# Memory read-out of an attention kernel: from one 128-row matmul per step to one 64-row matmul per head

## The chip, the cores and the metric

The kernel runs on one core of a Trainium2 chip. The metric is the device time of one execution in microseconds (us), lower is better. The profile comes from one profiled execution; the times of unprofiled executions are given beside it. The engines are named as in the profile: PE is TensorE (matmul and transpose), PEld its weight load, DVE is VectorE, ACT is ScalarE, POOL is GpSimd, SP is SyncE, which only issues DMA here.

## The reference, cut to what matters

Attention with a compressive memory, then two MLP layers on its output. B = 4, H = 8, S = 576, D = 64; 2304 tokens of width 512; the hidden width is 2048.

```python
scores = scale * q @ k.transpose(0, 1, 3, 2)            # causal mask, softmax -> a
local = a @ v
q_p = phi(q)                                            # elu(q) + 1
mem_ret  = einsum('bhsd,bhde->bhse', q_p, M_prev)       # the memory read-out:
mem_norm = einsum('bhsd,bhd->bhs', q_p, z_prev) + 1e-6  # 64 columns and one more
mem_out = mem_ret / mem_norm
attn = g * mem_out + (1 - g) * local                    # g = sigmoid(beta) per head
x = attn.transpose(0, 2, 1, 3).reshape(2304, 512)
x = silu(x @ moe_w_in) @ moe_w_out                      # layer 0
y = mish(x @ moe2_w_in) @ moe2_w_out                    # layer 1
```

## The kernel before

**Attention.** The 32 heads are taken as 16 pairs; the two heads of a pair (e = 0, 1) share the 128 partitions, 64 each, as q and k lie transposed. Queries come in tiles `qt` of 128 (the last, qt = 4, has 64). A visit is a pair with the tiles 0 and 1, or with 2, 3 and 4; the 32 visits make 80 steps (pair, qt), 64 with 128 queries and 16 with 64. A step has three parts. `stage_a` writes the scores to two PSUM banks (fp32 matmuls on 64 rows, one for each head), takes the softmax's exponent and moves the fp16 halves of P through a DMA that transposes. `stage_b`, three steps later (`LAG`), is the mix: six fp16 matmuls for each block of 128 keys and each head pair give local (64 columns and the sum of weights, 65), and **one fp32 matmul gives the memory read-out of both heads**: phi(q) of the pair (`er[v]`, 128 rows) times `rm[v]`, a 128 x 130 tile which holds M and z of head 0 in its upper left quarter, of head 1 in its lower right one, and zeros elsewhere. The step's 260 columns lie in one bank, 6 for an even and 7 for an odd qt. Behind an odd qt and qt 4 DVE divides and weighs (reciprocal, two products) and POOL adds memory and local to `x`. `stage_c` turns x on PE (line 609) into columns 260 on of the same banks; ACT copies both banks' parts out with one instruction, and a DMA writes them to `xd`.

**Layers.** Both layers run over 9 chunks of 256 tokens. A chunk of layer 0 is 384 fp16 matmuls of 256 columns ("gemms" below): `gemm1` (xh times w) and `gemm2` (g times w), 3456 in all; layer 1 has 1728 of 256 and 864 of 512 columns. Gemms of layer 0 fill PE between the steps of the attention. `hidden` is the activation between the two, `flush` takes a finished chunk out of PSUM.

**Weights.** The weights come as float64 bits; a `weight_unit` turns 1/16 of a layer's into fp32: DMA to a stage `ws`, ACT (Abs), DVE (shift), DVE (merge), ACT (low half), DVE (add), ACT (a Square with a sum, line 671). After eight units `weight_scale` finds the scale (DVE, a PE matmul of `diag`, DVE), and eight `weight_split` make fp16 halves (ACT, then DVE). Layer 1's fp32 weights lie in the arena that the attention's buffers have; so a unit of layer 1 can begin only where the part of the arena that it takes is free.

**What sets the order.** Nothing is scheduled on the chip. A planner (`Plan`) is given each operation with a cost and a priority, and writes a fixed order for every engine before the kernel is built; each engine then works through its row in order and waits where a semaphore says so. The price of a matmul goes by the rows it uses (line 372: a matmul on 64 rows is priced at half). An order is needed wherever two operations touch overlapping byte ranges, and `Plan.region` takes an access as one range from its first to its last byte: what spans banks 6 and 7 spans all that lies between.

```python
f1 = f0 + sum(st * (n - 1) for st, n in ap[1:]) + 1        # region(): one interval
```

Of the kernel before, what the change touches and what calls it, by code (L numbers as in the profile page):

```python
# [15 lines left out]
ALU = mybir.AluOpType  # L16
# [14 lines left out]
STEPS = [(v, qt) for v, (_, qts, _) in enumerate(VISITS) for qt in qts]  # L31
NS = len(STEPS)
PT_BLOCKS = 50
VM = 130 + NQ * 2 * (D + 1)
COLD = 50000.
XMAX, WMAX, OMAX = 8.0, 4.0, 64.0
PSCALE = 32768.0
# [140 lines left out]
def attn_moe_moe2_kernel(ctx: ExitStack, tc: tile.TileContext, kq, vm, beta, w1, w2, out):  # L178
# [26 lines left out]
    def ring(tiles):  # L205
        state = [0]

        def take():
            state[0] += 1
            return tiles[(state[0] - 1) % len(tiles)]  # L210

        return take
# [56 lines left out]
        return ts  # L269

    pt_tile, = carve([PT_BLOCKS, 128], F16)
    kqr, rmr, rvr = ring(carve([2, S], F32, 2)), ring(carve([130], F32, 3)), ring(carve([VM - 130], F32, 2))
    khr, klr = ring(carve([S], F32R, 2)), ring(carve([S], F32R, 2))
    q1r, q2r, q4s = ring(carve([256], F32, 2)), ring(carve([2, 256], F32R, 2)), carve([2, D], F32R, 2)
    v1s, v2s = carve([NQ, 2, D + 2], F16, 2), carve([NQ, 2, D], F16, 2)
# [62 lines left out]
    def ts(prio, out, in0, s1, op0, s2=None, op1=None):  # L338
        plan.add(prio, [c_ts(out, in0, s1, op0, s2, op1)], [out], aps(in0, s1), shared=not ps(in0))
# [53 lines left out]
    def setup():  # L393
        p = -1e9
        other(p, "SP", 100, lambda: nc.scalar.dma_start(out=gb, in_=beta), [gb])
        for x, t in enumerate(q4s):
            for r, e in ((slice(0, 64), 1), (slice(64, 128), 0)):
                o = t[r, e].bitcast(F32)
                plan.add(p + x, [
                    ("DVE", 0.52 * cols(o) + 68, lambda o=o: nc.vector.memset(o, 0.0)),  # L400
                    ("POOL", 1.0 * cols(o) + 60, lambda o=o: nc.gpsimd.memset(o, 0.0))], [t[r]], [])

        def consts():
            make_identity(nc, ident16)
            nc.gpsimd.memset(mask, 0.0)

            for r, c, n in ((slice(0, 128), 0, 128), (slice(0, 64), 128, D), (slice(64, 128), 128, D)):
                m = mask[r, c:c + n]
                nc.gpsimd.affine_select(
                    out=m, in_=m, compare_op=ALU.is_ge, fill=-1e9, base=0, pattern=[[-1, n]], channel_multiplier=1)  # L410
            make_identity(nc, ident)
            nc.gpsimd.memset(eps[:, 0:2], 1e-9 * PSCALE)
            nc.gpsimd.memset(eps[:, 2:4], 1e-6)
            nc.gpsimd.memset(ones, 1.0)
            nc.gpsimd.memset(onesf, 1.0)
            for t in scales:
                nc.gpsimd.memset(t[:, 2:4], 1.0)
# [24 lines left out]
    def load_vm(v, prio):  # L442
        p, _, nk = VISITS[v]
        n = nk * 2 * (D + 1)
        t, rm[v] = rvr()[:, 0:n], rmr()
        rv[v] = t.rearrange("p (n e d) -> p n e d", n=nk, e=2)
        dma(prio, t, vm[p, :, 130:130 + n], reads=[])
        dma(prio, rm[v], vm[p, :, 0:130], reads=[])

    def prep_q(v, j, prio):  # L450

# [21 lines left out]
    def prep_v(v, prio):  # L473
        nk = VISITS[v][2]
        r = rv[v]
        v1, v2 = v1r()[:, 0:nk, :, 0:D + 1], v2r()[:, 0:nk]
        x, top, scale, inv = r[:, :, :, 0:D], topr()[:, 0:1], scaler(), scr()
        other(prio, "DVE", 1.04 * nk * 2 * D + 146, lambda: nc.vector.tensor_reduce(
            out=top, in_=x, axis=mybir.AxisListType.XYZ, op=ALU.max, apply_absolute_value=True), [top], [x])
        total = bank[7][:, 400:401]  # L480
        mm(prio, [(total, ones, top, True, True)])
        ts(prio, inv[:, 0:2], total.to_broadcast([128, 2]), 2.0**-14, ALU.mult, 1e-30, ALU.max)
        ts(prio, inv[:, 0:2].bitcast(U32), inv[:, 0:2].bitcast(U32), 0x7F800000, ALU.bitwise_and)
# [433 lines left out]
```

## Time and profile before

| what | value |
|---|---|
| median of 3 runs | 1027.28 us (1027.22 to 1029.82) |
| the profiled execution | 1026.43 us, its span 1024.4 us |
| PE busy | 946.8 us, 92% of the span |
| DVE, ACT, POOL busy | 665.1, 645.4, 261.3 us (65, 63, 26%) |
| chain that ended last | PE 51%, issue 28%, POOL 8%, DVE 5%, ACT 4%, DMA 4% |
| fp32 read-outs of 130 columns in the trace | 128 records with 128 queries (34.1 us), 32 with 64 queries (6.6 us) |

The read-outs' busy time counts each of the two passes that an fp32 matmul makes from its start to its modelled end, and neighbours overlap; what a matmul costs PE is read from starts. The granted clock of PE is given as a share: 1.00 is 2.4 GHz, 0.50 is 1.2 GHz.

### The profile page before, as it was taken

Reading aid. Unit: us, or ns where it says so; the run is one execution under the profiler, and the core shown is the slowest. Engines: PE = TensorE matmul, PEld = TensorE weight load, DVE = VectorE, ACT = ScalarE, POOL = GpSimd, SP = SyncE. Lnnn points to the kernel's source line nnn. Section 1 sums busy time; section 2 is a strip of 40 time slices with the busy share of each in tenths; the row PEclk is TensorE's granted clock in tenths of the full one; section 3 lists DMA queues with packets and bytes.
Section 4 is the critical chain, followed back from the end, with each engine's and each line's share of the span. In section 5 each row is a group of like instructions: output and inputs, shape, how many; then the busy total and the mean of one; then the engine's idle time right before and its main releaser. Section 6 shows DMA issues by size and latency. Waiting matters only on the chain.

```text
span 1024.4 us, 20771 instructions
## 1 busy us (share of the span) xinstructions
PE 946.8 (92%) x8364; PEld 731.8 (71%) x8364; DVE 665.1 (65%) x1228; ACT 645.4 (63%) x1101; POOL 261.3 (26%) x279
## 2 busy tenths in 40 slices
PE   2437789999999999999999998999999999999996
PEld 1225678888888888888888886766666667666663
DVE  6988776777886878778769456753454544544441
ACT  7977766677766666677767675554455545555543
POOL 1111312332424224323223212222122211222211
PEclk9956889999999999999999998999999999999998
DMA  9757455666777576755451421010100101000000
GB/s 320 232 146 203 145 149 128 153 159 167 139 182 160 131 173 149 162 135 129 162 180 58 166 104 42 22 42 2 42 21 22 42 1 42 30 12 22 1 22 20
DMA packets 149904, 107.93 MB, mean 105 GB/s; under 512 B 111152, under 2 KB 139312, under 8 KB 145712
## 3 DMA queue, kind: packets, MB, share of 16 engines
q1 hardware_dynamic: 149664, 106.60, 39.0%
q8 instruction: 65, 1.06, 0.4%
q14 instruction: 31, 0.25, 0.1%
q10 hardware_dynamic: 144, 0.00, 0.0%
HBM read 66.21 MB, written 14.16 MB: 78 GB/s over the span
## 4 chain that ended last, share of the span: by engine, by line
PE 51%; issue 28%; POOL 8%; DVE 5%; ACT 4%; DMA 4%; SPq 0%; POOLq 0%; DVEq 0%; ACTq 0%
PE banks L374 50%; POOL g L327 8%; DVE w L321 1%; PE banks L609 1%; DMA g<-w 1%; ACT w L313 1%; ACT arena L313 1%; DVE arena L321 1%; DMA arena<-arena 1%; DMA xs<-yd 1%; DVE arena L327 1%; ACT ws L671 0%; DVE xh L321 0%; ACT ws L313 0%; ACT xh L313 0%
## 5 line engine op out<-in xcount | busy, mean ns | idle before, releaser
L374 PEld LDWEIGHTS <-w 128*128 128x128 f16 x3456 | 334.8, 98 | 42.8 <-issue 3.7
L374 PEld LDWEIGHTS <-arena 128*128 128x128 f16 (+1 forms) x3168 | 225.8, 101 | 78.7 <-DMA arena<-arena 26.7
L374 PE MATMUL banks<-g,w 128*128 128x256 f16 x1728 | 212.8, 275 | 2.6 <-POOL g L327 1.8
L327 POOL TENSOR_TENSOR g<-ga,g 128x512 f16<-128x512 f32 x107 | 136.5, 1275 | 298.4 <-ACT g L313 278.0
L374 PE MATMUL banks<-xh,w 128*128 128x256 f16 x1728 | 206.7, 273 | 0.0
L374 PE MATMUL banks<-xh,arena 128*128 128x256 f16 x1728 | 200.9, 274 | 2.4 <-ACT xh L313 1.3
L374 PE MATMUL banks<-arena,g 128*128 128x512 f16 x864 | 199.6, 381 | 3.1 <-ACT g L313 2.5
L374 PE MATMUL banks<-arena 128*128 128x65 f16 (+7 forms) x1728 | 115.7, 232 | 58.9 <-ACT arena L313 23.9
L374 PEld LDWEIGHTS <-g 128*128 128x128 f16 x864 | 84.8, 98 | 92.2 <-ACT g L313 3.0
L313 ACT ACTIVATE w<-w 128x512 f32<-128x512 f32 x108 | 67.8, 628 | 85.9 <-DVE w L318 57.3
L313 ACT ACTIVATE arena<-arena 128x256 f32<-128x256 f32 (+6 forms) x181 | 103.1, 593 | 17.6 <-PE banks L374 7.3
L321 DVE SCALAR_TENSOR_TENSOR arena<-arena 128x256 f16<-128x256 f32 (+6 forms) x144 | 108.0, 760 | 7.3 <-ACT arena L313 6.6
L321 DVE SCALAR_TENSOR_TENSOR ga<-ga,banks 128x512 f32<-128x512 f32 x108 | 73.8, 683 | 50.2 <-ACT ga L313 49.7
L313 ACT ACTIVATE arena<-banks,arena 128x128 f32<-128x128 f32 (+4 forms) x144 | 73.7, 547 | 33.6 <-DVE arena L545 32.2
L327 POOL TENSOR_TENSOR g<-w,g 128x512 f16<-128x512 f32 x36 | 41.7, 1157 | 184.0 <-ACT g L313 184.0
L313 ACT ACTIVATE ga<-ga 128x512 f32<-128x512 f32 x108 | 66.1, 626 | 34.5 <-DVE ga L321 18.1
L318 DVE TENSOR_SCALAR w<-banks,xsc 128x512 f32<-128x512 f32 x36 | 27.0, 751 | 87.1 <-PE banks L374 87.0
L545 DVE TENSOR_REDUCE arena<-banks 128x2 f32<-128x256 f32 (+3 forms) x80 | 64.2, 802 | 26.2 <-PE banks L374 23.9
L313 ACT ACTIVATE g<-ga 128x512 f16<-128x512 f32 x108 | 67.5, 626 | 18.0 <-DVE ga L321 13.5
L313 ACT ACTIVATE ga<-banks,xsc 128x512 f32<-128x512 f32 x72 | 49.4, 686 | 40.7 <-PE banks L374 38.3
L327 POOL TENSOR_TENSOR arena<-arena 128x256 f32<-128x256 f32 (+1 forms) x48 | 39.7, 826 | 130.5 <-DVE arena L327 86.8
L374 PEld LDWEIGHTS banks<-arena 128*128 128x128 f32 (+2 forms) x288 | 40.9, 223 | 33.6 <-ACT arena L313 30.5
(96 smaller groups left out, 928.8 us busy)
## 6 DMA issues: line engine op xcount, KB each, us to landing
ws<-w SPq DMA_DIRECT2D x28, 1024.0 KB, 5.2
arena<-kq SPq DMA_DIRECT2D x16, 576.0 KB, 4.4
arena<-vm SPq DMA_DIRECT2D x16, 325.0 KB, 3.2
xs<-xd SPq DMA_DIRECT2D x9, 512.0 KB, 4.6
yd<-w SPq DMA_DIRECT2D x36, 128.0 KB, 2.0
xs<-yd SPq DMA_DIRECT2D x9, 512.0 KB, 3.8
arena<-kq SPq DMA_DIRECT2D x16, 256.0 KB, 3.2
xd<-arena SPq DMA_DIRECT2D x32, 128.0 KB, 2.3
```

The costliest lines, as they stand in the source:

```text
L313: return ("ACT", ns, lambda: nc.scalar.activation(out=out, in_=in_, func=func, scale=scale, bias=bias))
L318: return ("DVE", ns, lambda: nc.vector.tensor_scalar(out=out, in0=in0, scalar1=s1, scalar2=s2, op0=op0, **kw))
L321: return ("DVE", 1.04 * cols(out) + 160, lambda: nc.vector.scalar_tensor_tensor(out=out, in0=in0, scalar=s, in1=in1, op0=op0, op1=op1))
L327: return (e, ns, lambda: eng.tensor_tensor(out=out, in0=in0, in1=in1, op=op))
L374: nc.tensor.matmul(out=o, lhsT=l, rhs=r, start=a, stop=z)
L545: other(prio, "DVE", 1.04 * cols(both) + 146, lambda: nc.vector.tensor_reduce(out=m1, in_=both, axis=AX, op=ALU.max, negate=True), [m1], [ ...
L609: plan.add(prio, [("PE", 56, lambda o=o, x2=x2: nc.tensor.transpose(o, x2, ident[0:R, 0:R]))], [o], [x2, ident], edge=(107, 56))
```

## The change

The read-out is done by head. Two fp32 matmuls take the place of the one: head e on rows 64e to 64e+63 of the array, 65 columns, and `rm` shrinks from 130 columns with zeros to 65 without (the DMA of it from 520 to 260 bytes a partition). Head e's results go to bank 6 + e, for local and memory; the parity of qt picks the columns, 0:130 or 130:260. The small vectors (`eps`, `scales`, `gv`) are interleaved to fit, the DVE and POOL work on the mix has as many elements in other access patterns, and x is written in another order. An even step, which wrote bank 6 alone, now writes both banks, and so does qt 4.

```diff
-kqr, rmr, rvr = ..., ring(carve([130], F32, 3)), ring(carve([VM - 130], F32, 2))
+kqr, rmr, rvr = ..., ring(carve([D + 1], F32, 3)), ring(carve([VM - D - 1], F32, 2))
...
-        dma(prio, t, vm[p, :, 130:130 + n], reads=[])
-        dma(prio, rm[v], vm[p, :, 0:130], reads=[])
+        dma(prio, t, vm[p, :, D + 1:D + 1 + n], reads=[])
+        dma(prio, rm[v], vm[p, :, 0:D + 1], reads=[])
...
     def stage_b(n, prio):
-        vb = bank[6 + qt % 2]
+        c0 = 130 * (qt % 2)
...
         for e in range(2):
-            o = vb[0:R, 65 * e:65 * e + 65]
+            o = bank[6 + e][0:R, c0:c0 + 65]
...
-        mm(prio, ms + [(vb[0:R, 130:260], er[v][:, 128 * qt:128 * qt + R], rm[v], True, True)])
+        for e in range(2):
+            r = slice(64 * e, 64 * e + 64)
+            ms.append((bank[6 + e][0:R, c0 + 65:c0 + 130], er[v][r, 128 * qt:128 * qt + R], rm[v][r], True, True))
+        mm(prio, ms)
         if not last(n):
             return
         m = 1 + qt % 2
-        g = banks[0:R, 512 * 6:512 * 8].rearrange("p (b c) -> p b c", b=2)[:, 0:m, 0:260].rearrange("p b (a c) -> p b a c", a=4)
-        den, t4, x = denr()[0:R, 0:m], t4r()[0:R, 0:m], xr()[0:R, 0:m]
-        each = lambda y: y[0:R].unsqueeze(1).to_broadcast([R, m, 4])
-        tt(prio, den, g[:, :, :, D], each(eps), ALU.add)
+        g = banks[0:R, 512 * 6:512 * 8].rearrange("p (e c) -> p e c", e=2)[:, :, 0:130 * m].rearrange("p e (a c) -> p e a c", c=65)
+        den, t4, x = denr()[0:R, :, 0:2 * m], t4r()[0:R, :, 0:2 * m], xr()[0:R, 0:m]
+        quad = lambda y: y.rearrange("p e (q k) -> p e q k", k=2)
+        each = lambda y: y[0:R].rearrange("p (e k) -> p e k", e=2).unsqueeze(2).to_broadcast([R, 2, m, 2])
+        tt(prio, quad(den), quad(g[:, :, :, D]), each(eps), ALU.add)
         other(prio, "DVE", 165, lambda: nc.vector.reciprocal(out=den, in_=den), [den], [den])
-        tt(prio, t4, g[:, :, :, 0:D], den.unsqueeze(3).to_broadcast([R, m, 4, D]), ALU.mult)
-        tt(prio, x, t4[:, :, 0:2], t4[:, :, 2:4], ALU.add, ("POOL", "DVE"))
+        tt(prio, t4, g[:, :, :, 0:D], den.unsqueeze(3).to_broadcast([R, 2, 2 * m, D]), ALU.mult)
+        t4 = t4.rearrange("p e (q k) d -> p e q k d", k=2)
+        tt(prio, x.rearrange("p q e d -> p e q d"), t4[:, :, :, 0], t4[:, :, :, 1], ALU.add, ("POOL", "DVE"))
```

The planner writes another order for it. Three places follow, as the instructions of one engine stand in its row; `arena_98` holds all buffers of the attention, `w_73` layer 0's weights. Names in the first and second place carry the buffer's number alone, in the third a second number too.

PE, a mix with qt = 1 in the middle of the attention, before: the last fp16 matmuls, the read-out (128 x 130), and a gemm behind it.

```order
L374 LDWEIGHTS arena_98
L374 MATMUL banks<-arena_98 128x64
L374 LDWEIGHTS arena_98
L374 MATMUL banks<-arena_98 128x65
L374 MATMUL banks<-arena_98 128x130
L374 LDWEIGHTS w_73
L374 MATMUL banks<-g_76,w_73 128x256
```

PE, a mix with qt = 2 in the changed kernel: three matmuls of 65 columns stand together, the last of local in fp16 and the two read-outs, and behind them those of the next step.

```order
L374 MATMUL banks<-arena_98 128x65
L374 LDWEIGHTS arena_98
L374 MATMUL banks<-arena_98 128x64
L374 LDWEIGHTS arena_98
L374 MATMUL banks<-arena_98 128x65 x3
L374 LDWEIGHTS arena_98
L374 MATMUL banks<-arena_98 128x65
L374 LDWEIGHTS arena_98
L374 MATMUL banks<-arena_98 128x64
```

One read-out of 130 columns became two of 65, and the mix of the odd step stands directly behind that of the even one, where gemms stood.

PE, a mix with qt = 4 (64 queries), with what its first instructions wait for, before and then changed. `DMAHW6` is the DMA that transposes P.

```order
L374 MATMUL banks_63<-arena_r_0_97 128x64 x2
L374 LDWEIGHTS ident16_0_67
L374 MATMUL banks_63<-mask_0_68,ident16_0_67 128x64
L374 LDWEIGHTS arena_0_98 [waits DMAHW6_49]
L374 MATMUL banks_63<-arena_0_98 64x65 [waits DVE_49]
L374 LDWEIGHTS arena_0_98
L374 MATMUL banks_63<-arena_0_98 64x64
```

```order
L374 LDWEIGHTS w_0_73
L374 MATMUL banks_63<-g_0_76,w_0_73 128x256
L374 LDWEIGHTS w_0_73
L374 MATMUL banks_63<-g_0_76,w_0_73 128x256
L374 LDWEIGHTS arena_0_98 [waits DMAHW6_49]
L374 MATMUL banks_63<-arena_0_98 64x65 [waits Activation_49]
L374 LDWEIGHTS arena_0_98
L374 MATMUL banks_63<-arena_0_98 64x64
```

The first matmul waited for DVE, which had read the bank's mix before; it now waits for ACT, whose copy in `stage_c` of the step group ahead takes the transposed x out of both banks. The transposes that this copy waits for stand 18 gemms ahead (15 of them behind the last one).

ACT, the end of layer 0, before: `ga_80<-banks` and `g_76<-ga_80` are parts of `hidden`, `L671` the Square of a weight unit of layer 1, `arena_98,wsc_0_93` a split of layer 1's weights, `w_73<-banks,xsc_91` the last flush of layer 0, `xh_75<-xs_74`, the input of layer 1's first chunk, stands directly behind these rows.

```order
L671 ACTIVATE ws_78,topw_0_88<-arena_98 128x1024
L313 ACTIVATE ga_80<-banks,xsc_91 128x512
L313 ACTIVATE g_76<-ga_80 128x512
L313 ACTIVATE arena_98<-arena_98,wsc_0_93 128x1024 x2
L313 ACTIVATE ga_79<-banks,xsc_91 128x512
L313 ACTIVATE arena_98<-arena_98,wsc_0_93 128x1024 x2
L313 ACTIVATE g_76<-ga_79 128x512
L313 ACTIVATE ga_80<-banks,xsc_91 128x512
L313 ACTIVATE arena_98<-arena_98,wsc_0_93 128x1024 x2
L313 ACTIVATE g_76<-ga_80 128x512
L313 ACTIVATE arena_98<-arena_98,wsc_0_93 128x1024 x2
L313 ACTIVATE w_73<-banks,xsc_91 128x256 x2
```

The same place in the changed kernel; the Square has line 677 here, `arena_98<-ws_77` is the Abs at the head of a weight unit.

```order
L677 ACTIVATE ws_78,topw_0_88<-arena_98 128x1024
L313 ACTIVATE g_76<-ga_80 128x512
L313 ACTIVATE arena_98<-ws_77 128x1024
L313 ACTIVATE ws_77<-ws_77 128x1024
L313 ACTIVATE w_73<-banks,xsc_91 128x256 x2
L313 ACTIVATE arena_98<-ws_78 128x1024
L677 ACTIVATE ws_77,topw_0_88<-arena_98 128x1024
L313 ACTIVATE w_73<-banks,xsc_91 128x256 x2
L313 ACTIVATE ws_78<-ws_78 128x1024
L677 ACTIVATE ws_78,topw_0_88<-arena_98 128x1024
L313 ACTIVATE arena_98<-arena_98,wsc_0_93 128x1024
L313 ACTIVATE xh_75<-xs_74,xsc_89 128x1024
```

Before, all sixteen units of layer 1 and the second scale were done ahead of the layer's last hidden activations. Now the last two units, the scale and the first split stand between the last flushes and `xh_75`. On PE the last read-out stands behind 2484 gemms of layer 0 where it stood behind 2208, the last transpose behind 2511 where it was 2235, and the second `diag` of layer 1's weights behind all 3456 where it was 3330. In front of the first gemm2 the order of the instructions on PE, DVE and SP is nearly the old one; behind the switch 126 matmuls of layer 1's gemm1 stand ahead of its first gemm2 where 93 stood.

## Rows read from the trace of the kernel before

**Rows 1.** Busy time by stretch: us, then PE, PEld, DVE, ACT, POOL, PEclk, DMA, GB/s.

```profile
121.00:138.00 17.00, 10.28 (x63) 7.72 (x64) 14.60 (x39) 11.94 (x22) 3.53 (x5) 0.50 0.71 196
...
400.00:490.00 90.00, 90.00 (x1063) 75.85 (x1060) 68.07 (x136) 59.94 (x110) 32.31 (x35) 1.00 0.64 146
...
626.30:629.70 3.40, 3.40 (x18) 2.35 (x17) 3.40 (x7) 2.85 (x4) 2.21 (x1) 0.50 0.00 0
```

**Rows 2.** Timeline of PE, 152 to 160 us: start, us, engine, line, operation, count.

```profile
152.29 1.69 PE L374 MATMUL banks<-g,w 128*128 128x256 f16 x14
153.82 0.65 PE L374 MATMUL banks<-arena 128*128 128x65 f16 x8
154.31 0.82 PE L374 MATMUL banks<-g,w 128*128 128x256 f16 x6
...
155.53 0.49 PE L374 MATMUL banks<-g,w 128*128 128x256 f16 x3
155.95 0.70 PE L374 MATMUL banks<-arena 64*128 64x256 f32 x4
156.59 0.28 PE L374 MATMUL banks<-mask,ident 128*128 128x128 bf16 x2
...
158.02 0.83 PE L374 MATMUL banks<-arena 128*128 128x65 f16 x14
158.69 0.49 PE L374 MATMUL banks<-g,w 128*128 128x256 f16 x3
159.10 0.49 PE L374 MATMUL banks<-arena 64*128 64x128 f32 x4
159.53 0.28 PE L374 MATMUL banks<-mask,ident 128*128 128x128 bf16 x2
```

**Rows 3.** Timeline of ACT: one of the last copies of transposed x (stage_c).

```profile
477.85 0.39 ACT L313 ACTIVATE arena<-banks 128x256 f32<-128x256 f32 x1 [1.75 <-PE banks L609]
```

**Rows 4.** Timeline of PE: the last mix of the attention, and the layer switch.

```profile
488.54 1.39 PE L374 MATMUL banks<-arena 128*64 128x65 f16 x32
489.86 0.33 PE L609 MATMUL banks<-ident,arena 128*128 128x128 f32 x1
...
614.02 0.39 PE L374 MATMUL banks<-diag,onesf 128*128 128x128 f32 x2
...
625.90 6.85 PE L374 MATMUL banks<-g,w 128*128 128x256 f16 x46 [1.79 <-POOL g L327]
634.06 0.27 PE L374 MATMUL banks<-xh,arena 128*128 128x256 f16 x1 [1.31 <-ACT xh L313]
```

**Rows 5.** Timeline of ACT, the last unit of layer 1's weights and the switch.

```profile
602.62 1.13 ACT L313 ACTIVATE arena<-ws 128x1024 f32<-128x1024 f32 x1 [2.05 <-DMA ws<-w]
...
610.87 1.14 ACT L671 ACTIVATE ws<-arena 128x1024 f32<-128x1024 f32 x1
...
615.93 2.19 ACT L313 ACTIVATE arena<-arena,wsc 128x1024 f16<-128x1024 f32 x2 [1.53 <-DVE wsc L318]
...
632.13 0.84 ACT L313 ACTIVATE w<-banks,xsc 128x256 f32<-128x256 f32 x2 [2.77 <-PE banks L374]
632.86 1.15 ACT L313 ACTIVATE xh<-xs,xsc 128x1024 f16<-128x1024 f32 x1
```

**Rows 6.** Timeline of DVE, the same unit and the scale behind it.

```profile
600.61 0.69 DVE L318 TENSOR_SCALAR arena<-arena 128x1024 uint32<-128x1024 uint32 x1 [2.60 <-ACT arena L313]
601.34 1.22 DVE L321 SCALAR_TENSOR_TENSOR arena<-ws,arena 128x1024 uint32<-128x1024 uint32 x1
...
609.62 1.21 DVE L327 CUSTOM_DVE_ANT_0 arena<-ws,arena 128x2048 uint16<-128x2048 uint16 x1
612.12 0.16 DVE L330 TENSOR_REDUCE mx<-topw 128x1 f32<-128x8 f32 x1 [1.29 <-ACT ws L671]
...
614.66 0.28 DVE L330 TENSOR_REDUCE cvec<-banks 128x1 f32<-128x128 f32 x1
...
615.74 0.15 DVE L318 TENSOR_SCALAR wsc<-wsc 128x1 f32<-128x1 f32 x1
```

More of the change, by code (lines that the diff above doesn't have):

```diff
@@ L33 @@
 PT_BLOCKS = 50
-VM = 130 + NQ * 2 * (D + 1)
+VM = D + 1 + NQ * 2 * (D + 1)
 COLD = 50000.
@@ L271, in attn_moe_moe2_kernel @@
     pt_tile, = carve([PT_BLOCKS, 128], F16)
-    kqr, rmr, rvr = ring(carve([2, S], F32, 2)), ring(carve([130], F32, 3)), ring(carve([VM - 130], F32, 2))
+    kqr, rmr, rvr = ring(carve([2, S], F32, 2)), ring(carve([D + 1], F32, 3)), ring(carve([VM - D - 1], F32, 2))
     khr, klr = ring(carve([S], F32R, 2)), ring(carve([S], F32R, 2))
@@ L411, in consts @@
             make_identity(nc, ident)
-            nc.gpsimd.memset(eps[:, 0:2], 1e-9 * PSCALE)
-            nc.gpsimd.memset(eps[:, 2:4], 1e-6)
+            nc.gpsimd.memset(eps[:, 0:4:2], 1e-9 * PSCALE)
+            nc.gpsimd.memset(eps[:, 1:4:2], 1e-6)
             nc.gpsimd.memset(ones, 1.0)
@@ L416, in consts @@
             for t in scales:
-                nc.gpsimd.memset(t[:, 2:4], 1.0)
+                nc.gpsimd.memset(t[:, 1:4:2], 1.0)
             for t in v1s:
@@ L423, in setup @@
         g3 = gb.rearrange("p (a h) -> p a h", h=2)
-        ts(p, gv[:, :, 0:2], g3, -0.5, ALU.mult, 0.5, ALU.add)
-        ts(p, gv[:, :, 2:4], g3, 0.5, ALU.mult, 0.5, ALU.add)
+        ts(p, gv[:, :, 0:4:2], g3, -0.5, ALU.mult, 0.5, ALU.add)
+        ts(p, gv[:, :, 1:4:2], g3, 0.5, ALU.mult, 0.5, ALU.add)
     rq, rk, rv, rm, kk, vv, qq, er = {}, {}, {}, {}, {}, {}, {}, {}
@@ L481, in prep_v @@
         mm(prio, [(total, ones, top, True, True)])
-        ts(prio, inv[:, 0:2], total.to_broadcast([128, 2]), 2.0**-14, ALU.mult, 1e-30, ALU.max)
-        ts(prio, inv[:, 0:2].bitcast(U32), inv[:, 0:2].bitcast(U32), 0x7F800000, ALU.bitwise_and)
+        ts(prio, inv[:, 0:4:2], total.to_broadcast([128, 2]), 2.0**-14, ALU.mult, 1e-30, ALU.max)
+        ts(prio, inv[:, 0:4:2].bitcast(U32), inv[:, 0:4:2].bitcast(U32), 0x7F800000, ALU.bitwise_and)
         other(prio, "DVE", 160, lambda: nc.vector.reciprocal(out=scale, in_=inv[:, 0:1]), [scale], [inv])
@@ L588, in stage_b @@
         m = 1 + qt % 2
-        g = banks[0:R, 512 * 6:512 * 8].rearrange("p (b c) -> p b c", b=2)[:, 0:m, 0:260].rearrange("p b (a c) -> p b a c", a=4)
-        den, t4, x = denr()[0:R, 0:m], t4r()[0:R, 0:m], xr()[0:R, 0:m]
-        each = lambda y: y[0:R].unsqueeze(1).to_broadcast([R, m, 4])
-        tt(prio, den, g[:, :, :, D], each(eps), ALU.add)
+        g = banks[0:R, 512 * 6:512 * 8].rearrange("p (e c) -> p e c", e=2)[:, :, 0:130 * m].rearrange("p e (a c) -> p e a c", c=65)
[3 more added lines that the diff above has]
+        tt(prio, quad(den), quad(g[:, :, :, D]), each(eps), ALU.add)
         other(prio, "DVE", 165, lambda: nc.vector.reciprocal(out=den, in_=den), [den], [den])
-        tt(prio, den, den, each(gvv), ALU.mult)
-        tt(prio, t4, g[:, :, :, 0:D], den.unsqueeze(3).to_broadcast([R, m, 4, D]), ALU.mult)
-        tt(prio, x, t4[:, :, 0:2], t4[:, :, 2:4], ALU.add, ("POOL", "DVE"))
+        tt(prio, quad(den), quad(den), each(gvv), ALU.mult)
+        tt(prio, t4, g[:, :, :, 0:D], den.unsqueeze(3).to_broadcast([R, 2, 2 * m, D]), ALU.mult)
+        t4 = t4.rearrange("p e (q k) d -> p e q k d", k=2)
+        tt(prio, x.rearrange("p q e d -> p e q d"), t4[:, :, :, 0], t4[:, :, :, 1], ALU.add, ("POOL", "DVE"))
         xts[n] = (x, R)
@@ L889 @@
     vp = vp.reshape(NP, 2, NQ, 128, D + 1).transpose(0, 3, 2, 1, 4)
-    mz = np.zeros((NP, 2, D, 2, D + 1), f32)
-    for e in range(2):
-        mz[:, e, :, e, :D] = np.asarray(M_prev).reshape(NP, 2, D, D)[:, e]
-        mz[:, e, :, e, D] = np.asarray(z_prev).reshape(NP, 2, D)[:, e]
+    mz = np.concatenate([np.asarray(M_prev).reshape(NP, 128, D), np.asarray(z_prev).reshape(NP, 128, 1)], 2)
     def weights(wi, wo):
@@ L902 @@
         "kq": np.concatenate([pair_t(np.asarray(k)), pair_t(np.asarray(q))], 2),
-        "vm": np.concatenate([mz.reshape(NP, 128, 130), vp.reshape(NP, 128, NQ * 2 * (D + 1))], 2),
+        "vm": np.concatenate([mz, vp.reshape(NP, 128, NQ * 2 * (D + 1))], 2),
         "betar": np.ascontiguousarray(np.broadcast_to(np.asarray(beta), (128, H))),
```

## The prediction

> **What bounds the kernel now.** I read the busy time by stretch first, since the average (PE busy 92%) mixes stages [rows 1]. Up to 138 us the weights are being prepared and PE waits: in the last part of that, 121 to 138 us, it works 10.28 of 17 us at the half clock. From there to the end of the attention PE is the bound: 400 to 490 us shows 90.00 of 90.00 at the full clock, with ACT at 59.94 and DVE at 68.07. So in that stretch a nanosecond more on PE is a nanosecond of the kernel, and work of ACT, DVE and POOL is hidden. At the layer switch PE has gaps of 1.79 and 1.31 us [rows 4]. The timeline of PE then gives prices from start to start (a row's own duration includes the pipeline's drain), the timelines of ACT and DVE the chain at the switch.
>
> **Part 1, the read-out itself.** Before: 14 gemms from 152.29 to 153.82 make 0.109 us each [rows 2]. The group of 8 (six fp16 matmuls and the two passes of the read-out) lasts 0.49 us to the next start, that of 14 (twelve and two) 0.67. The difference is six fp16 matmuls, 0.18, so the read-out takes 0.31 of the 0.49.
>
> After: the trace has no 65-column pair on 64 rows, but the scores of `stage_a` are such pairs, with 256 and 128 columns [rows 2]. Their four records are two heads by two passes. The pair of 256 columns takes 0.64 us (155.95 to 156.59), that of 128 takes 0.43 (159.10 to 159.53). That is 0.21 for 128 columns more; at 65 columns it makes 0.43 - 63 x 0.00164 = 0.33. Most of it doesn't depend on columns, so halving them saves little. And the array goes from 128 rows to 64 for it: the three gemms ahead of a pair last 0.42 and 0.41 (155.53 to 155.95, 158.69 to 159.10) where three take 0.33. So 0.09 comes on top: 0.42 for the new read-out against 0.31, **0.11 more for a step with 128 queries**. A row that would give a gain: by columns alone the pair saves 65 x 0.00164 = 0.107 a step. That is the lower bound, -0.11; the upper one is heads one behind the other instead of side by side, another 0.32, +0.43. I take +0.11, since it is the only one that adds up from rows of the same shape of array. With 64 queries the array is already on half its columns: 1.32 us from 488.54 to 489.86 for 30 fp16 matmuls and the read-out [rows 4]; less 30 x 0.03, the read-out takes 0.42 as it is, and the new one 0.42 too. I take 0 there (-0.1 to +0.1).
>
> The Trainium skill weighs in for the change here: TensorEngine Tiling (Array Packing), section Theoretical Speedup, gives "Up to 2×" where a small dimension is at most 64. By that 0.31 would become 0.16, and 48 such steps would give 7 us back. The pairs of the rows say otherwise, and the same page's Key Properties has a reason: changing the tiling mode drains TensorE.
>
> Of the 80 steps, 16 stand in the start, where PE waits for weights anyway: they cost nothing as long as these come last (if not, 16 x 0.11, doubled at the half clock, 3.5). Of the other 64, 48 have 128 queries: **48 x 0.11 = 5.3 us** (-5 to +21).
>
> **Part 2, the same bank waits.** An even step now writes both banks and so waits for ACT's copy of the group before, which spans them. The order shows 27 mixes that wait for ACT where 16 did, and behind the wait on PE stand all gemms. The copy takes 0.39 us [rows 3], and may be queued behind an ACT instruction of up to 1.15. Between the transposes and the wait stand mostly 9 to 24 gemms, 1.0 to 2.6 us, with 4 to 7 in three places. Before, waits with 9 or 10 gemms ahead lie in the stretch that shows 100% for PE [rows 1]. So most are covered; three short ones at up to 1 us bound it at 3. I take 0.5.
>
> **Part 3, the order and the layer switch.** The wait is in the planner's account too, and the attention's end moves from behind 2208 layer-0 gemms to behind 2484: 276 x 0.109 = 30 us later. PE's sum of work doesn't change by that. What hangs on it are the weights of layer 1, whose fp32 lies in the attention's arena. Before, the last unit's Square ends at 612.0, and scale and splits go on in the shadow of 20 us of gemms [rows 4 to 6]; `xh` follows the first flush at once: flush starts 632.13, first gemm of layer 1 at 634.06, 1.93 us. In the changed order the last unit, the scale and a split stand on ACT between that flush and `xh`, and ACT takes its row in order. On the path, then, behind the flush's start: flush 0.84, Abs 1.13, DVE 0.69 and 1.22, add 1.21, Square 1.14, the scale, split 1.10 (half of 2.19), `xh` 1.15 [rows 5, 6]. The scale is 0.16 on DVE, 0.39 on PE [rows 4], and 1.23 from 614.66 to 615.89 on DVE: 1.8 at least. From 612.12 to 615.89 it took 3.8, but there its matmul stood behind gemms, which it would not here; I take 2.4, for the product of `diag` and the handovers. Sum 10.9, and 0.6 for six more handovers: 11.5 instead of 1.93, **+9.6** (9.0 to 11.0 by the scale's bounds).
>
> Against it: before, layer 0's tail had a wait of 1.79 us for the activation, which stood behind splits [rows 4], and 3.40 us at the half clock after it [rows 1], which cost half of that, 1.7. In the new order those splits come later, so up to 3.5 may come back. I take 1.5 of it, because the units that now stand there occupy ACT and DVE in the same way. After the longer gap the clock may be low for such a stretch again, 0 to +1.7; I take 0, since the old switch ends in a gap as well. Another check: if the units keep their pace behind the attention, the last Square comes 30 + 5.3 us later, at 647.4, and the first gemm of layer 1 at 652, +18. The order packs the last units closer than that, so this is the upper end. In layer 1 more gemm1 stand ahead of the first gemm2 (126 for 93), 3.6 us of cover for the splits that now fall there; I take nothing for them.
>
> **Costs at nothing.** DVE and POOL do the same number of elements on the mix, under a PE that is full (if they were the bound, some tenths for 32 groups). The DMA of `rm` halves; DMA is at 0.64 in the full stretch and waits on nothing there. The start keeps its order, so 138 stays.
>
> **Sum.** 5.3 + 0.5 + 9.6 - 1.5 = 13.9. On the profiled execution's 1026.43 that is 1040.3; the median of the runs lies 0.85 above that execution, so **1041.2**. Bounds of this case: 5.3 + 9.6 - 3.5 = 11.4 (1038) to 18 + 3 (1048).
>
> **Rivals.** *The switch absorbs it*: the last units come early enough, since the real chip runs the units faster than the planner, and only part 1 remains, 1027.3 + 5.3 = 1032.6. For it: ACT was idle for 2.77 us ahead of the flush [rows 5]. Against it: ACT's row is fixed, so the Abs behind the flush can't go ahead of it. *Nothing to be measured* (within 0.3%, 1024.2 to 1030.4): as that, and the waits and half clock of the tail come back, 5.3 - 3.5 = +1.8, 1029. *Faster*: the two halves stream side by side without the 0.09 at their entry and save the columns, 0.107 a step on 64 steps, -6.8, and the switch doesn't move: 1020.5. It decides from where the entry and the fixed part of a pair together fall below 0.2; what speaks against it is that all pairs in the trace show 0.33 and 0.09. *Much slower*: the heads' halves don't run side by side when they write banks 6 and 7, 48 x 0.32 = 15 more, or the ACT waits don't hide: 1050 to 1060. That the halves of the scores start together speaks against the first.
>
> **How the numbers follow.** The forecast's case 0.68, the switch absorbs it 0.11, nothing 0.05, faster 0.06, much slower 0.10. The forecast is the likeliest one's 1041. The range takes in the forecast's case and the absorbed switch, 1032 to 1050; outside are the other cases, some 0.2. A measurement of this kernel can tell about 0.3%, 3 us, from no change: slower 0.68 + 0.11 + 0.10 = 0.89, same 0.05, faster 0.06.
>
> **What would show it.** Part 1: pairs of 65 columns on 64 rows with 0.33 us from their start to the next, and 0.09 more in the gemm ahead; starts of the two heads within some ns. Part 2: idle time of PE with ACT as releaser ahead of a mix, under 3 us in all from 140 to 540. Part 3: the first gemm of layer 1 at 645 to 650 us, ahead of it a gap of PE of some 11 us with Abs, add, Square, `diag` in it, and the last mix near 524. The prediction is wrong if the gap at the switch is under 4 us, or if the mixes take as long as before.

## The result, and the profile after

The changed kernel takes 1040.53 us (median of 4 runs, 1037.34 to 1043.23) where the kernel before takes 1028.55 (4 runs beside it). The ratio is 1.013, with a 95% interval of 1.0108 to 1.0152: 13 us slower (11 to 16); the two medians alone lie 12.0 apart. The prediction was 1041, with 1032 to 1050 as its range.

The profiled execution took 1043.23 us, the upper end of its runs, with a span of 1041.4 against 1024.4. So the two traces differ by 17 us where the medians differ by 12 to 13. Four times read from the starts in the timeline of PE cut both spans into stretches; the third is called the gap below:

| stretch | before | after | difference |
|---|---|---|---|
| start to the first gemm2 of layer 0 | 134.8 | 132.5 | -2.3 |
| from there to the last gemm of layer 0 | 497.6 | 504.8 | +7.1 |
| from there to the first gemm of layer 1 | 1.6 | 12.6 | +11.0 |
| from there to the last instruction of PE | 384.9 | 385.8 | +0.9 |

Busy time of the changed kernel by stretch; the columns are those of [rows 1]:

```profile
400.00:490.00 90.00, 90.00 (x1028) 75.33 (x1025) 63.44 (x127) 57.25 (x106) 29.14 (x35) 1.00 0.59 125
...
637.30:649.90 12.60, 1.86 (x8) 1.05 (x6) 6.94 (x21) 7.76 (x13) 0.00 (x0) 0.72 0.12 42
649.90:652.00 2.10, 0.92 (x4) 0.50 (x4) 2.10 (x3) 2.08 (x2) 0.00 (x0) 0.50 0.00 0
652.00:655.00 3.00, 3.00 (x16) 2.13 (x14) 1.87 (x2) 2.67 (x4) 0.00 (x0) 0.50 0.63 175
```

The full stretch of PE is as full as it was [rows 1]; what is added there is work and not waiting. The new hole is the second row: in 12.6 us PE works 1.86. The granted clock behind it is 0.50, half, until at least 655.

The timeline of PE in the changed kernel, two mixes in the attention and the switch:

```profile
341.93 2.27 PE L374 MATMUL banks<-arena 128*128 128x65 f16 x50
344.13 0.50 PE L374 MATMUL banks<-g,w 128*128 128x256 f16 x3
...
524.78 1.40 PE L374 MATMUL banks<-arena 128*64 128x65 f16 x34
526.11 3.12 PE L374 MATMUL banks<-g,w 128*128 128x256 f16 x27
...
632.37 5.18 PE L374 MATMUL banks<-g,w 128*128 128x256 f16 x46 [1.31 <-POOL g L327]
644.67 0.79 PE L374 MATMUL banks<-diag,onesf 128*128 128x128 f32 x2 [7.12 <-DVE diag L327]
645.85 0.80 PE L374 MATMUL banks<-diag,onesf 128*128 128x128 f32 x2 [0.38 <-DVE diag L327]
649.88 0.37 PE L374 MATMUL banks<-xh,arena 128*128 128x256 f16 x1 [3.24 <-ACT xh L313]
651.44 11.05 PE L374 MATMUL banks<-xh,arena 128*128 128x256 f16 x77 [1.19 <-DVE xh L321]
```

The group of 50 is the mix with qt = 2 and that with qt = 3 one behind the other: 42 fp16 matmuls and eight records of read-outs (two steps, two heads, two passes), 2.20 us to the next start. The last mix starts at 524.78, where it was 488.54 [rows 4]. At the switch PE waits 7.12 us for the `diag` of the second weight scale and 3.24 for `xh`.

ACT at the switch, to be read against [rows 5]:

```profile
636.93 0.84 ACT L313 ACTIVATE w<-banks,xsc 128x256 f32<-128x256 f32 x2 [1.59 <-PE banks L374]
637.66 1.12 ACT L313 ACTIVATE arena<-ws 128x1024 f32<-128x1024 f32 x1
638.66 1.15 ACT L677 ACTIVATE ws<-arena 128x1024 f32<-128x1024 f32 x1
...
639.77 0.84 ACT L313 ACTIVATE w<-banks,xsc 128x256 f32<-128x256 f32 x2
640.49 1.12 ACT L313 ACTIVATE ws<-ws 128x1024 uint32<-128x1024 uint32 x1
642.90 1.12 ACT L677 ACTIVATE ws<-arena 128x1024 f32<-128x1024 f32 x1 [1.29 <-DVE arena L327]
...
647.64 1.15 ACT L313 ACTIVATE arena<-arena,wsc 128x1024 f16<-128x1024 f32 x1 [3.55 <-DVE wsc L318]
648.70 1.13 ACT L313 ACTIVATE xh<-xs,xsc 128x1024 f16<-128x1024 f32 x1
```

And DVE beside it, to be read against [rows 6]:

```profile
638.81 0.69 DVE L318 TENSOR_SCALAR arena<-arena 128x1024 uint32<-128x1024 uint32 x1 [1.10 <-ACT arena L313]
639.54 1.23 DVE L321 SCALAR_TENSOR_TENSOR arena<-ws,arena 128x1024 uint32<-128x1024 uint32 x1
641.64 1.23 DVE L327 CUSTOM_DVE_ANT_0 arena<-ws,arena 128x2048 uint16<-128x2048 uint16 x1 [0.88 <-ACT ws L313]
644.13 0.16 DVE L330 TENSOR_REDUCE mx<-topw 128x1 f32<-128x8 f32 x1 [1.26 <-ACT ws L677]
...
647.46 0.15 DVE L318 TENSOR_SCALAR wsc<-wsc 128x1 f32<-128x1 f32 x1
```

From the flush at 636.93 to the first gemm of layer 1 at 649.88 runs one chain: Abs, shift, merge, low half, add, Square, the scale from 644.13 to 647.61, split, `xh`. Before, flush and `xh` alone took 1.93 us.

### The profile page after: what moved, and what is told of

It is laid out like the page before. It is cut to its first block, busy times and chain, and to the rows that moved or that the text cites. A ratio compares the mean times of both kernels' runs of the same rounds, so it can differ in the third digit from the quotient of the medians.

```text
span 1041.4 us, 21099 instructions
## 1 busy us (share of the span) xinstructions
PE 959.9 (92%) x8524; PEld 735.4 (71%) x8524; DVE 661.9 (64%) x1224; ACT 646.2 (62%) x1102; POOL 268.7 (26%) x282
## 4 chain that ended last, share of the span: by engine, by line
PE 49%; issue 27%; POOL 8%; DMA 5%; DVE 5%; ACT 5%; SPq 0%; POOLq 0%; DVEq 0%; ACTq 0%
PE banks L374 48%; POOL g L327 8%; DMA ws<-w 2%; DVE w L321 1%; ACT w L313 1%; DMA yd<-w 1%; ACT arena L313 1%; ACT ws L677 1%; DVE arena L321 1%; DMA g<-w 1%; PE banks L615 1%; DVE arena L327 1%; ACT ws L313 1%; DVE ga L321 0%; DMA arena<-arena 0%
## 5 line engine op out<-in xcount | busy, mean ns | idle before, releaser
L374 PEld LDWEIGHTS <-w 128*128 128x128 f16 x3456 | 330.6, 98 | 47.2 <-issue 5.5
L374 PE MATMUL banks<-xh,w 128*128 128x256 f16 x1728 | 209.3, 274 | 1.3 <-DVE xh L321 0.7
L327 POOL TENSOR_TENSOR g<-ga,g 128x512 f16<-128x512 f32 x108 | 132.8, 1230 | 293.3 <-ACT g L313 289.6
L374 PE MATMUL banks<-arena 128*64 128x65 f16 (+6 forms) x1888 | 118.8, 237 | 34.7 <-ACT arena L313 22.0
L313 ACT ACTIVATE arena<-arena 128x256 f32<-128x256 f32 (+6 forms) x185 | 105.3, 595 | 17.0 <-PE banks L374 7.9
L327 POOL TENSOR_TENSOR arena<-arena 128x256 f32<-128x256 f32 (+1 forms) x48 | 42.7, 890 | 120.9 <-DVE arena L327 90.1
L374 PEld LDWEIGHTS banks<-arena 64*128 64x128 f32 (+1 forms) x448 | 40.3, 211 | 37.1 <-ACT arena L313 29.8
```

The costliest lines, as they stand in the source:

```text
L313: return ("ACT", ns, lambda: nc.scalar.activation(out=out, in_=in_, func=func, scale=scale, bias=bias))
L327: return (e, ns, lambda: eng.tensor_tensor(out=out, in0=in0, in1=in1, op=op))
L374: nc.tensor.matmul(out=o, lhsT=l, rhs=r, start=a, stop=z)
```

## The experiments

Two things were to be told apart: what the read-out costs on the array, and what the order of the engines costs at the switch. All ratios are against the kernel before, run beside on the same chip (its median is 1028.55 beside the changed kernel and 1025.2 to 1026.3 beside the others). The stretches are those of the table above, each from one trace; the last column is the time from the first gemm2 to the last instruction of PE, so without the start, which the column first gemm2 holds. Before and before_own_diag, whose totals agree, lie 2.3 us apart in it, so a difference of that size in one trace tells nothing.

| kernel | ratio (95% interval) | first gemm2 | to last layer-0 gemm | gap | rest | behind the start |
|---|---|---|---|---|---|---|
| before | 1 | 134.8 | 497.6 | 1.6 | 384.9 | 884.1 |
| changed | 1.013 (1.0108 to 1.0152) | 132.5 | 504.8 | 12.6 | 385.8 | 903.1 |
| before_told | 1.0057 (1.0037 to 1.0076) | 132.5 | 495.8 | 12.6 | 385.1 | 893.5 |
| layout_128rows | 1.0117 (1.0098 to 1.0136) | 132.9 | 511.4 | 1.6 | 382.9 | 895.8 |
| after_no_span | 1.0155 (1.0132 to 1.0179) | 138.6 | 510.5 | 1.6 | 384.0 | 896.1 |
| after_own_diag | 1.0062 (1.0041 to 1.0084) | 131.6 | layer 1 starts 7.3 us before it ends | | | 892.1 |
| after_twice | 1.0297 (1.0274 to 1.032) | 136.6 | 515.7 | 12.7 | 384.4 | 912.8 |
| after_price | 1.0143 (1.0119 to 1.0167) | 127.7 | 511.9 | 9.4 | 385.1 | 906.4 |
| before_own_diag | 0.9999 (0.9986 to 1.0013) | 134.5 | 495.8 | 1.6 | 384.4 | 881.8 |
| told_own_diag | 0.9948 (0.9928 to 0.9969) | 130.0 | layer 1 starts 6.2 us before it ends | | | 884.7 |
| before_fp16 | 1.0017 (1.0001 to 1.0033) | 137.0 | 490.2 | 11.8 | 385.9 | 887.9 |
| before_fp16_own_diag | 0.9916 (0.9893 to 0.9939) | 133.8 | 489.4 | 0.1 | 384.9 | 874.4 |

**before_told: the order without the read-out.** The planner of the kernel before is told of writes that don't happen, so it writes the order that the new layout asks for.

```diff
-        mm(prio, ms + [(vb[0:R, 130:260], ...)])
+        mm(prio, ms + [(vb[0:R, 130:260], ...)],
+           also=[bank[6 + e][0:R, 130 * (qt % 2):130 * (qt % 2) + 130] for e in range(2)])
...
-        plan.add(prio, [("PE", ns, go)], writes, ...)
+        plan.add(prio, [("PE", ns, go)], writes + list(also), ...)
```

> The kernel before, its read-out and banks untouched; only the planner is told that each mix also writes its 130 columns in both banks, so it writes the order that goes with the new layout (last mix behind 2454 layer-0 gemms, the second diag of layer 1's weights behind all 3456). Theory (order and array are separate terms): nothing of the read-out's price, the gap at the layer switch as in the changed kernel, some 11 us before the first gemm of layer 1 instead of 1.6: +9 to +11, 1037 to 1039. Rival (the array alone makes the difference): within 3 us of before, 1026 to 1031.

Ratio 1.0057, some 6 us, and not the 9 to 11 of the expectation. The gap is there to the tenth (12.6 us), with the same wait for `diag`, in the timeline of PE:

```profile
635.61 0.79 PE L374 MATMUL banks<-diag,onesf 128*128 128x128 f32 x2 [7.11 <-DVE diag L327]
...
640.82 0.37 PE L374 MATMUL banks<-xh,arena 128*128 128x256 f16 x1 [3.23 <-ACT xh L313]
```

So the gap belongs to the order and needs no 64-row matmul. What the expectation left out is that in this trace the stretch ahead of the gap is 1.9 us shorter and the start 2.3; behind the start the kernel is 9.4 us longer. The difference to the changed kernel, in the stretch ahead of the gap, is 504.8 - 495.8 = 9.0 us: that comes with the read-out, against 7.9 us by its starts (below). Here, too, a mix with qt = 2 and one with qt = 3 stand one behind the other, with the old read-out and gemms behind them:

```profile
228.61 2.03 PE L374 MATMUL banks<-arena 128*128 128x65 f16 x46
230.48 1.80 PE L374 MATMUL banks<-xh,w 128*128 128x256 f16 x15
```

The two last 1.87 us to the next start, where the changed kernel has 2.20: 0.165 more a step.

**layout_128rows: by head, on 128 rows.** The banks of the changed kernel, but `rm` keeps its zeros and each head's 65 columns are computed on all rows.

```diff
         for e in range(2):
-            r = slice(64 * e, 64 * e + 64)
-            ms.append((bank[6 + e][0:R, c0 + 65:c0 + 130], er[v][r, ...], rm[v][r], True, True))
+            ms.append((bank[6 + e][0:R, c0 + 65:c0 + 130], er[v][:, ...], rm[v][:, 65 * e:65 * e + 65], True, True))
```

> The changed kernel's banks, but each head's read-out on all 128 rows (rm keeps its zeros, 65 columns each): two fp32 matmuls without a change from 128 rows to 64. Its order has the last mix behind 2325 gemms and the second weight diag behind 3417. Theory (entering and leaving 64 rows costs some 0.09 each): the group of read-outs is 0.31 to 0.40 us from start to next, under the 0.46 to 0.5 of the changed kernel; gap at the switch 2 to 5 us; 1029 to 1035. Rival (splitting by head costs, however many rows): read-out at 0.46 or more, 1036 or more.

Ratio 1.0117: the rival is right on the read-out. By the median starts of its four passes they lie 0.138, 0.112, 0.112 and 0.112 us apart, 0.47 in all where the old read-out has 0.192 and 0.112. The last pass costs 0.112 at 130 columns and at 65; the first is shorter at 65, 0.138 for 0.192, but there are four passes for two. In the rows, the same pair of mixes as above lasts 2.20 us, as in the changed kernel:

```profile
378.28 2.36 PE L374 MATMUL banks<-arena 128*128 128x65 f16 x50
380.48 0.49 PE L374 MATMUL banks<-g,w 128*128 128x256 f16 x3
```

Splitting by head therefore costs about 0.17 us a step with or without a change of rows. Of the 13.7 us that the stretch is longer than before, 48 x 0.17 = 8.2 are the read-outs, and PE is idle in it for 6.6 us where it was 3.3; the other 2.2 stay open. The theory's gap of 2 to 5 us came out at 1.6.

**after_no_span: no copy across the mix.** x is transposed into columns 384:512 of bank 6 and 0:128 of bank 7, so ACT's copy no longer spans a mix.

```diff
-            o = bank[6 + e][0:R, c0:c0 + 65]
+            o = bank[6 + e][0:R, c0 + 128 * e:c0 + 128 * e + 65]
...
-            ..., bank[6 + i][:, 260:260 + R]
+            ..., banks[:, 3456 + 128 * i:3456 + 128 * i + R]
```

> The changed kernel with 64-row read-outs, but x is transposed into the last 128 columns of bank 6 and the first 128 of bank 7, head 1's mix moves to columns 128:388 of bank 7, so ACT's copy spans no mix and the even mix doesn't wait for it. The order has the last mix behind 2334 gemms, the second weight diag behind 3432. Theory: the read-outs keep their +0.16 us on 48 steps (+7.7), the switch gap shrinks to 2 to 5 us: 1033 to 1038. Rival (the gap comes from PE's longer work, not from the wait): as the changed kernel, 1039 to 1042.

Ratio 1.0155, not faster than the changed kernel; the theory's total failed. Its parts held better: the gap is 1.6 us, the attention ends behind fewer gemms, and behind the start the kernel is 7.0 us shorter than the changed one. But the same chain now stands some gemms ahead of the end of layer 0 and not behind it, and stops PE there, in the timeline of PE:

```profile
627.23 2.46 PE L374 MATMUL banks<-xh,w 128*128 128x256 f16 x21
...
640.33 0.82 PE L374 MATMUL banks<-xh,w 128*128 128x256 f16 x6
643.60 0.49 PE L374 MATMUL banks<-diag,onesf 128*128 128x128 f32 x2 [2.45 <-DVE diag L327]
643.92 0.38 PE L374 MATMUL banks<-g,w 128*128 128x256 f16 x2
644.89 0.37 PE L374 MATMUL banks<-g,w 128*128 128x256 f16 x1 [0.59 <-POOL g L327]
645.05 0.78 PE L374 MATMUL banks<-diag,onesf 128*128 128x128 f32 x2
645.63 3.74 PE L374 MATMUL banks<-g,w 128*128 128x256 f16 x21
650.67 0.27 PE L374 MATMUL banks<-xh,arena 128*128 128x256 f16 x1 [1.31 <-ACT xh L313]
```

PE waits 2.45 us, and the 21 gemms from 645.63 take 3.74 where the 21 from 627.23 take 2.46. What takes the total back is the start, 6.1 us longer than the changed kernel's; why, I don't know. Removing the wait moved the chain and shortened what it costs, but didn't remove it.

**after_own_diag: one buffer.** In the program the first chunk of layer 1 takes its `diag` from a ring of two. Two calls earlier in that ring, on the same buffer, stands the second weight scale of layer 1, so the chunk's scale, and with it `xh`, must wait until the weights are scaled. The edit gives the chunk a buffer in a part of the weight tile that is free then.

```diff
-        d = diagr()
+        d = diagr() if d is None else d
...
-        largest(prio, p, top, spot)
+        largest(prio, p, top, spot, d=spares[2][:, 0:128] if (l, c) == (1, 0) else None)
```

> The changed kernel with one edit: the first chunk of layer 1 has a diag buffer of its own (in a part of the weight tile that is free then) instead of the one in turn, so its scale and xh need not follow the second scale of layer 1's weights. The order is the same up to the end of the attention. Theory (the chain of weight unit, scale and split in front of xh is the gap): first gemm of layer 1 1.5 to 4 us behind the last of layer 0 instead of 12.6, then 306 gemm1 ahead of the first gemm2: 1030 to 1034. Rival (layer 1 waits for the weights anyway and the gap only moves in front of its first gemm2): 1038 to 1042.

Ratio 1.0062: 7 us of the 13 come back by this edit, and the total lies where the theory put it. Layer 1 doesn't start 1.5 to 4 us behind layer 0, as expected, but at 632.07, before layer 0 has ended:

```profile
632.07 3.89 PE L374 MATMUL banks<-xh,arena 128*128 128x256 f16 x33
639.43 7.04 PE L374 MATMUL banks<-xh,arena 128*128 128x256 f16 x63
648.24 0.49 PE L374 MATMUL banks<-diag,onesf 128*128 128x128 f32 x2 [1.76 <-DVE diag L327]
```

The wait for the weights' `diag` is now 1.76 us, since 96 gemms of layer 1 cover it. In the traces, behind the start, 11.0 of the 19.0 us are gone, and the 8.0 that are left agree with the 7.9 that the read-outs cost by their starts (below).

**after_twice: the pair a second time.** Each pair is issued twice in a row; the second writes the same result.

```diff
-            for o, l, r, a, z in ms:
+            pair = [m for m in ms if m[1].shape[0] == 64 and cols(m[0]) == 65]
+            for o, l, r, a, z in ms + pair:
```

> The changed kernel with each pair of read-outs issued a second time right behind the first, in the same order otherwise. A second pair enters no new mode, so it gives the price of two passes of two heads alone. Theory (a pass costs a fixed 0.155 to 0.16 us at 65 columns on 64 rows, side by side for both heads, besides 0.09 at the entry and 0.05 at the exit): 0.31 to 0.33 us more from the first to the next start, 48 x 0.32 + 16 x 0.21 = 19 us over the changed kernel behind 138 us. Rival (entering and leaving 64 rows is the whole price, passes go by columns): a second pair at under 0.2 us, under 10 us more.

Neither number was right; the pair's 0.22 us lies between them. By the rows, the two mixes last 2.65 us where the changed kernel has 2.20, for two more pairs:

```profile
373.89 2.72 PE L375 MATMUL banks<-arena 128*128 128x65 f16 x58
376.54 0.50 PE L375 MATMUL banks<-g,w 128*128 128x256 f16 x3
```

A pair within the mode costs 0.22 us, 0.111 a pass for both heads side by side, which is the price of a pass on 128 rows. The starts of the pair in the changed kernel are 0.122 behind the last fp16 matmul (0.029 without a change of rows), 0.161 from the first pass to the second, and 0.210 from the second to the next instruction. So of 0.493 only 0.222 is two passes; 0.27 is entering, the first weight load and leaving. The old read-out has 0.029 + 0.192 + 0.112 = 0.333, of which 0.224 is two passes. The stretch grew by 10.9 us (by the starts 48 x 0.222 = 10.7, and 1.9 for qt = 4), the total by 16 to 17, of which 4.1 lie at the start.

**after_price: the planner's price.** Each pass of a pair is priced 62 ns higher.

```diff
-                ns += (one + ...) * l.shape[0] / 128
+                ns += (one + ...) * l.shape[0] / 128 + (62 if l.shape[0] == 64 and n == 65 else 0)
```

> The changed kernel, with 62 ns more for each of the four passes of a pair in the planner's account, which prices a matmul on 64 rows at half. The order has the last mix behind 2367 gemms instead of 2484, but the second weight diag still behind all 3456. Theory (the chain behind the last layer-0 gemm is the gap, wherever the attention ends): gap at the switch 10 to 13 us, total within 4 us of the changed kernel, 1036 to 1043. Rival (the late end of the attention makes the gap): gap under 6 us, 1030 to 1035.

Ratio 1.0143, with a gap of 9.4 us, a little under the theory's 10 to 13. The last mix stands 117 gemms earlier than in the changed kernel, and the gap is there all the same, since the second weight `diag` still stands behind all gemms of layer 0, in the timeline of PE:

```profile
644.13 0.49 PE L374 MATMUL banks<-diag,onesf 128*128 128x128 f32 x2 [4.27 <-DVE diag L327]
649.03 0.37 PE L374 MATMUL banks<-xh,arena 128*128 128x256 f16 x1 [3.23 <-ACT xh L313]
```

The orders taken together say the same: with one `diag` ring for both, the gap is 1.6 us where this matmul stands behind 3330, 3417 or 3432 gemms (before, layout_128rows, after_no_span), and 9.4 to 12.7 where it stands behind all 3456.

**before_own_diag.** The edit of after_own_diag on the kernel before.

> The kernel before with a diag buffer of its own for the first chunk of layer 1. Its order has the second weight diag behind 3330 gemms anyway, and the chain in front of xh wasn't late. Theory: no change, 1023 to 1029, gap at the switch 0.5 to 2 us. Rival (the gap of any order is won back by it): 3 to 5 us less.

Ratio 0.9999 (0.9986 to 1.0013): no change, as the theory says. What the buffer holds up is free in the old order.

**told_own_diag.** The same edit on before_told.

> The kernel before in the order that goes with the new layout, with the diag buffer of its own. Theory (three terms that add: read-out +8, gap +11, and an order that loses 4 less ahead of the gap): told was 6 over before and loses the gap of 11, of which the changed kernel won back 7 by the same edit: -2 to -5, 1021 to 1024. Rival (the edit only works where the attention is longer): within 2 us of the told kernel without it, 1030 to 1033.

Ratio 0.9948: 5 us faster than before, 11 faster than before_told, near what the theory has. Layer 1 begins ahead of the wait for `diag`, in the timeline of PE:

```profile
622.73 3.77 PE L374 MATMUL banks<-xh,arena 128*128 128x256 f16 x33
637.55 0.49 PE L374 MATMUL banks<-diag,onesf 128*128 128x128 f32 x2 [1.52 <-DVE diag L327]
```

The gap goes with that one buffer: behind the start the kernel is 8.8 us shorter than before_told. That it is faster than the kernel before is another matter. In the traces this lies in the start, 130.0 for 134.8; behind it both take the same (884.7 and 884.1). So the late end of the attention costs nothing once the gap is gone; that it is the better order is not shown.

**before_fp16_own_diag and before_fp16: fewer and shorter passes.** Since an fp32 pass is dear (0.192 and 0.112 in the old read-out), phi(q) and `rm` are split into fp16 halves, and three fp16 matmuls of 130 columns replace the fp32 one, in the old layout.

```diff
+        rh[v], rl[v] = rhr(), rlr()
+        copy(prio, rh[v], rm[v])
+        rest(prio, rl[v], rm[v], rh[v])
...
+        copy(prio, h, e)
+        rest(prio, el[v][:, 64 * i0:64 * i1], e, h)
...
-        mm(prio, ms + [(vb[0:R, 130:260], er[v][:, 128 * qt:128 * qt + R], rm[v], True, True)])
+        mm(prio, ms + [(o, eh[v][:, q], rh[v], True, False), (o, eh[v][:, q], rl[v], False, False),
+                       (o, el[v][:, q], rh[v], False, True)])
```

> The kernel before with the read-out in fp16: phi(q) and rm are split into two fp16 halves (ACT or DVE, and POOL) and the 130 columns take three fp16 matmuls, on 128 rows, and with the diag buffer of its own. Theory (an fp32 matmul costs by its passes, 0.19 + 0.11, and an fp16 one of 130 columns about 0.055): read-out 0.17 instead of 0.31, 64 x 0.14 = 9 us less behind 138 us, as long as the splits' some 1.5 us a visit on the other engines stay hidden: 1016 to 1021. Rival (the splits make P or the mix late): 1026 to 1035.

> The fp16 read-out without the diag buffer of its own; its order has the second weight diag behind all 3456 gemms, 126 gemm1 ahead of the first gemm2, as the changed kernel's. Theory: the read-out's gain of 8 us stays and the gap of 9 to 12.6 us at the switch comes back: 1024 to 1030, the same as before. Rival (the gap is the changed kernel's own): 1015 to 1020.

With the buffer of its own the ratio is 0.9916: 8.6 us faster than the kernel before, the fastest here, as expected. By the starts its three passes take 0.056, 0.057 and 0.058 us, 0.171 in all for the old 0.304. The two mixes last 1.60 us:

```profile
393.36 1.77 PE L375 MATMUL banks<-arena 128*128 128x65 f16 x48
394.96 0.82 PE L375 MATMUL banks<-g,w 128*128 128x256 f16 x6
```

Without it, 1.0017, as expected: the read-outs' gain is there (490.2 in the stretch) and the gap as well (11.8), in the timeline of PE:

```profile
633.76 0.80 PE L375 MATMUL banks<-diag,onesf 128*128 128x128 f32 x2 [6.27 <-DVE diag L328]
638.97 0.37 PE L375 MATMUL banks<-xh,arena 128*128 128x256 f16 x1 [3.23 <-ACT xh L314]
```

So the gap isn't the changed kernel's own; a third order has it too.

## Why the prediction was right, point by point

**Part 1, mechanism right, size too small.** The forecast was +0.11 us a step, 5.3 us; the starts show 0.493 against 0.333, +0.16, and +0.014 for qt = 4 (0.390 against 0.376): 48 x 0.16 + 16 x 0.014 = 7.9 us. The entry was right (0.122 - 0.029 = 0.093 for 0.09). The step that was too small is the line through the pairs of 256 and 128 columns to 65, "at 65 columns it makes 0.43 - 63 x 0.00164 = 0.33". The pair takes 0.161 + 0.210 = 0.37. Its last pass lasts 0.204 from the second head's start whether it has 65 columns or 128, as the pairs of `stage_a` with 128 columns show in the same trace. Its first pass did follow the line, 0.161 for 0.214 at 128 columns. Two points on a line don't show where the line ends; the nearest row, 0.43 at 128 columns, would have been about as far off on the other side.

The rule on small dimensions that the prediction weighed, "Up to 2×" in the Trainium skill's TensorEngine Tiling (Array Packing), section Theoretical Speedup, doesn't come out here. The heads do run side by side: a pair costs 0.22 in the mode, the four passes on 128 rows 0.47. But one matmul with zeros needed only two passes for both heads, and a change of mode comes on top: 0.093 us at the entry, and at the exit 0.204 for a pass of 0.111, again 0.093. The drain that the page's Key Properties names would fit these, but the traces show only the times and not their reason.

**Part 2, right.** Taken at 0.5 us, bounded by 3. From 138 to 530 us PE is busy 391.95 of 392, and from 140 to 540 no wait of PE has ACT as its releaser. The distances to ACT's copy suffice, the short ones too.

**Part 3, right, and larger by 1.4 us.** The gap grew by 11.0 us where the sum had +9.6; from the flush's start to the first gemm 12.95 where it had 11.5. Two terms were short. The low half on ACT was left out of the chain: in the row it stood behind the other unit's Square and the second flush (640.49), and DVE's add waited 0.88 for it. And the scale took 3.5 us (644.13 to 647.61) and not 2.4, as the chunk's scale shares DVE and PE with it and the clock is low: `diag` takes 0.79 where it took 0.39 [rows 4]. The cause, the chain in ACT's row, is shown by after_own_diag and told_own_diag. That it hangs on one `diag` buffer wasn't seen in the prediction, which put it down to the end of the attention and to ACT's fixed row: in after_own_diag the attention ends as late as in the changed kernel, and the gap is gone. after_price has that end 117 gemms earlier and keeps most of the gap.

**What should come back** was taken at 1.5 us of 3.5. before_told is 1.9 shorter in that stretch, and the changed kernel, without its read-outs, 0.8 (7.1 - 7.9 = -0.8). The low clock behind the gap was put at 0 (bound 1.7); the rest of the span is 0.9 longer.

**Costs at nothing.** The start was taken to stay; in this trace it is 2.3 us shorter, in the others between 127.7 and 138.6. This was not pursued, and stays open. The traces' sum, -2.3 + 7.1 + 11.0 + 0.9, is 16.7, against the forecast's 13.9; by the medians and the ratio it is 12 to 13. So that the forecast's 1041 lies within 1 us of the median is in part luck: the two main terms were 2.6 and 1.4 us too small, and against them stand the start and the medians, which lie closer together than the two traces.

**The rivals.** That the switch absorbs it fails on the 12.6 us; that the heads run one behind the other fails on their starts, 7 ns apart; that nothing is to be measured fails on the interval, 1.0108 to 1.0152. *Faster* wanted the entry and the fixed part of a pair to be small: halving the columns does take 0.054 off the first pass (layout_128rows), but the entry costs 0.093 and the pair 0.37 where the two old passes take 0.304. Of *Much slower*, the waits for ACT fail on Part 2.

## What to carry to other kernels

Before a matmul is split to leave out zeros, count the passes and the changes of mode, and only then the columns: here the last fp32 pass costs the same 0.11 us at 65 and at 130 columns, so two heads in one matmul with zeros (0.30) are cheaper than two halves (0.46 on 64 rows, 0.47 on 128), and three fp16 passes of 0.057 are cheaper still. This holds for so few columns; the scores' pairs on 64 rows take 0.64 at 256 columns and 0.43 at 128 [rows 2]. When an edit in one place lengthens a gap far away, look for the chain that stands in it and ask of each link what it truly needs: here a ring of two scratch buffers tied the input of layer 1 to the scale of its weights, and one more buffer gave back 7 to 11 us in each of the three orders that had the gap.

## What was not expected of the hardware

A pair of fp32 matmuls on 64 rows costs 0.111 us a pass within its mode (after_twice), and as much the last pass of one matmul on 128 rows (0.112), at 65 columns (layout_128rows) as at 130 (before). Leaving the 64-row mode takes 0.204 us from the last start at 65 columns and at 128, in the changed kernel's trace; at 256 columns it takes 0.308. And a pass for 64 queries at 64 columns of the array is shorter: 0.059 in a second pair, and 0.058 in layout_128rows between two heads.
